# First feed-forward product of six token chunks as seven block products, a key maximum as bias, and a new order table

## The chip, the cores and the metric

The kernel runs on one core of one Trainium2 chip. Its engines work side by side, each through its own instructions in a fixed order: TensorE (PE) multiplies matrices out of SBUF into the eight banks of PSUM, VectorE (DVE) and ScalarE (ACT) work elementwise on either memory, GpSimd (POOL) on SBUF alone, and SyncE (SP) issues the DMA transfers to and from HBM. An instruction starts when the one before it on its engine has started or ended and the semaphores that it waits for have come. The metric is the device time of one execution in microseconds (us); lower is better.

## What is computed

Two stages. Linear attention with an exponential feature map, for 8 batches and 8 heads of 576 positions with 64 dimensions, and then a feed-forward part with a cosine:

```python
def phi(x):
    proj = einsum('bhsd,df->bhsf', x, w_phi)                  # 64 -> 128 features
    proj = proj - max(abs(proj), axis=-1, keepdims=True)
    return concatenate([exp(proj), exp(-proj)], axis=-1)
q_p, k_p = phi(q), phi(k)
kv  = einsum('bhsf,bhsd->bhfd', k_p, v);  z = sum(k_p, axis=2)
attn = einsum('bhsf,bhfd->bhsd', q_p, kv) / (einsum('bhsf,bhf->bhs', q_p, z) + 1e-6)
x = attn as (4608 tokens, 512)
h = x @ w_in                                                  # 512 -> 2048
out = (h * cos(h)) @ w_out                                    # 2048 -> 512
```

All of it is float32 in and out. The feed-forward weights are kept as 64-bit floats by the host and arrive as pairs of words.

## The kernel before

**Attention.** A unit is one batch and two heads; there are 32 units (`attention`, u = 0 to 31). A unit projects queries (L426, L429) and keys (L472, L496), takes the maximum of the absolute values, subtracts it, exponentiates both signs, multiplies with the values (L570, L576), then forms the denominators (L609) and the numerators (L619), and writes its part of x to HBM. For keys the maximum is a reduction on DVE (`k_max`, L508). For units 0 to 7 (`K_SUMS`) it is subtracted by a matmul with minus the unit matrix into the same bank (`k_sub`, L518); for the others by a DVE subtraction (L513). The key parts i = 0 and 1 are 128 x 512, part 2 is a tail of 128 x 128. The exponentials (`exp_k`, L526) then run on ACT, one instruction for a part and a sign. These matmuls have float32 operands, and the profile records each of them as two passes.

**Weights.** `convert` turns 16 tiles of the words (one tile: 128 features of w_in and of w_out) into a high and a low part of a shorter type, so that a product is three matmuls (high x high, low x high, high x low). Three of its operations, each over 1024 columns, are on POOL for tiles 0 to 3 (`W_POOL`) and on DVE for the others. The converted tiles lie in a ring of eight (`w`) and are stored to HBM; `reload` brings them back (1024 KB each).

**Feed-forward.** The 4608 tokens are 9 chunks of 512 (`visit`). Chunks 0 to 2 are visited several times, for a quarter or two of the weights at a time, while attention and conversion go on; chunks 3 to 8 once each, over all 16 weight tiles (stage "n."). For a chunk x is split into a high and a low part (L49 on ACT, L54 on DVE), and for each weight tile of 128 features come: the first product, 12 matmuls of 128 x 512 into one bank (`mm1`, L726: 4 blocks of the 512 inputs, three times); two ACT copies of the bank (`copy`, L732 to an integer number of turns, L733 as it is); `reduce` (DVE, L737), `cosine` (ACT, L741), `times` (DVE, L744), and the split of the result into `high` (ACT) and `low` (DVE); and the second product, 12 matmuls of 128 x 512 into four accumulating banks (`mm2`, L760 to L762). At the end of a chunk the four banks are copied out and stored.

**What sets the order.** Every piece of work is a `Step` with its engine and the steps that it needs. The table `ORDER` lists all steps of all engines in one sequence; each engine runs its own in that sequence, and the eight PSUM banks are given out along it. The number beside each step (its cost) is not used when the program is built. SP issues loads, stores and reloads in the same sequence.

## Time and profile before

| what | value |
|---|---|
| median of 3 runs | 1079.09 us (1079.06 to 1081.62) |
| profiled execution: span | 1079.3 us, 19379 instructions |
| PE matmuls recorded | 7614, of which 1728 in L726 and 1728 in L760 to L762 |
| HBM read, written | 118.55 MB, 41.94 MB |
| DMA packets | 92603, 161.76 MB, mean 150 GB/s |
| ACT table loads | 21 at the cosine, 11 and 9 at the exponentials, 1 at the first copy, 1283 ns each |

The profile has no time of the execution beside its span; the span is from the first instruction to the last. In the views below a row of the timeline is: start in us from the beginning of the span, duration in us, engine, line, operation, what is written <- what is read, and the shape; "PEld" is the weight load, which overlaps the matmuls. Numbers of buffers are left out of names where they tell nothing. A matmul's duration is longer than its share of the engine, since matmuls follow each other in a pipeline; its pitch is the distance of two starts.

### The profile page before, as it was taken

The page shows a single profiled execution, that of the slowest core. Times are in us where ns is not written, and L with a number is a line of the kernel's source. Part 1 is how long each engine was busy: PE and PEld are TensorE (multiplying, and loading weights), DVE is VectorE, ACT ScalarE, POOL GpSimd, SP SyncE. Part 2 cuts the span into 40 slices and gives each one's busy share as a digit, 9 for nine tenths or more (in the row PEclk, how much of TensorE's full clock was granted, in tenths as well). Part 3 has the DMA queues.
Part 4 walks back from the last instruction along what each step waited for, and adds up shares of the span by engine and source line. Part 5 has one row for each costly group of instructions (what it writes and reads, how often), then busy time and mean ns, then how long its engine had stood idle before and what let it go on. Part 6 is the DMA issues. An engine that isn't in the chain of part 4 may idle for free.

```text
span 1079.3 us, 19379 instructions
## 1 busy us (share of the span) xinstructions
PE 1071.7 (99%) x7614; PEld 828.3 (77%) x7614; DVE 704.1 (65%) x1139; ACT 710.7 (66%) x1352; POOL 157.3 (15%) x187
## 2 busy tenths in 40 slices
PE   9999999999999999999999999999999999999998
PEld 6657677787878877788677877786877878888886
DVE  5999999988788767634766556665756343424433
ACT  5898999778666676745676575867467644444442
POOL 3775223000000201101120111120111000000000
PEclk9999999999999999999999999999999999999999
DMA  7564754657655336473132733166312620620441
GB/s 214 174 183 151 221 158 123 199 180 255 219 197 171 118 119 227 177 251 137 54 116 95 234 134 113 41 215 214 97 32 83 232 100 30 244 97 1 174 158 59
DMA packets 92603, 161.76 MB, mean 150 GB/s; under 512 B 43744, under 2 KB 52064, under 8 KB 84320
## 3 DMA queue, kind: packets, MB, share of 16 engines
q1 hardware_dynamic: 92352, 160.46, 44.3%
q8 instruction: 60, 0.98, 0.4%
q14 instruction: 31, 0.25, 0.1%
q10 hardware_dynamic: 160, 0.07, 0.0%
HBM read 118.55 MB, written 41.94 MB: 149 GB/s over the span
## 4 chain that ended last, share of the span: by engine, by line
PE 92%; DVE 0%; issue 0%; DMA 0%; ACT 0%; DVEq 0%
PE bank L726 36%; PE bank L760 12%; PE bank L762 12%; PE bank L761 12%; PE bank L619 5%; PE bank L570 4%; PE bank L609 3%; PE bank L426 2%; PE bank L472 2%; PE bank L576 1%; PE bank L429 1%; PE bank L496 1%; DMA out<-o_last 0%; DVE w_t_f__961 L350 0%; PE bank L518 0%
## 5 line engine op out<-in xcount | busy, mean ns | idle before, releaser
L741 ACT ACT_TABLE_LOAD x21 | 26.9, 1283 | 0.3
L457 POOL COPY m_u__3949<-m_u__3949 32x36 f32<-32x36 f32 x3 | 2.4, 808 | 159.5 <-DVE m_u__3949 L452 159.5
L800 DVE TENSOR_TENSOR o<-bank,o 128x512 f32<-128x512 f32 x24 | 16.2, 684 | 4.0 <-PE bank L762 4.0
L531 ACT ACT_TABLE_LOAD x11 | 14.1, 1283 | 0.2
L726 PE MATMUL bank<-xh_c__5603,w 128*128 128x512 f32 x32 | 13.2, 411 | 0.0
L726 PE MATMUL bank<-xh_c__6807,w 128*128 128x512 f32 x32 | 12.9, 404 | 0.0
L726 PE MATMUL bank<-xh_c__7487,w 128*128 128x512 f32 x32 | 12.8, 399 | 0.0
L726 PE MATMUL bank<-xh_c__4406,w 128*128 128x512 f32 x32 | 12.6, 395 | 0.0
L726 PE MATMUL bank<-xh_c__5779,w 128*128 128x512 f32 x32 | 12.5, 391 | 0.0
L726 PE MATMUL bank<-xh_c__5689,w 128*128 128x512 f32 x32 | 12.5, 391 | 0.0
L726 PE MATMUL bank<-xh_c__6990,w 128*128 128x512 f32 x32 | 12.5, 391 | 0.0
L726 PE MATMUL bank<-xh_c__6870,w 128*128 128x512 f32 x32 | 12.5, 390 | 0.0
L726 PE MATMUL bank<-xh_c__5852,w 128*128 128x512 f32 x32 | 12.5, 390 | 0.0
L726 PE MATMUL bank<-xh_c__8046,w 128*128 128x512 f32 x32 | 12.5, 390 | 0.0
L726 PE MATMUL bank<-xh_c__6988,w 128*128 128x512 f32 x32 | 12.5, 390 | 0.0
L726 PE MATMUL bank<-xh_c__7887,w 128*128 128x512 f32 x32 | 12.5, 390 | 0.0
L726 PE MATMUL bank<-xh_c__4453,w 128*128 128x512 f32 x32 | 12.5, 389 | 0.0
L726 PE MATMUL bank<-xh_c__4662,w 128*128 128x512 f32 x32 | 12.5, 389 | 0.0
L726 PE MATMUL bank<-xh_c__4490,w 128*128 128x512 f32 x32 | 12.5, 389 | 0.0
L726 PE MATMUL bank<-xh_c__7907,w 128*128 128x512 f32 x32 | 12.4, 389 | 0.0
L726 PE MATMUL bank<-xh_c__8323,w 128*128 128x512 f32 x32 | 12.4, 389 | 0.0
L726 PE MATMUL bank<-xh_c__8787,w 128*128 128x512 f32 x32 | 12.4, 389 | 0.0
(3968 smaller groups left out, 4066.7 us busy)
## 6 DMA issues: line engine op xcount, KB each, us to landing
w<-w_parts SPq DMA_DIRECT2D x48, 1024.0 KB, 5.4
w_parts<-w SPq DMA_DIRECT2D x16, 1024.0 KB, 5.7
vmain<-vS SPq DMA_DIRECT2D x32, 256.0 KB, 4.1
out<-o SPq DMA_DIRECT2D x32, 256.0 KB, 2.9
sums<-o SPq DMA_DIRECT2D x24, 256.0 KB, 3.4
o<-sums SPq DMA_DIRECT2D x24, 256.0 KB, 3.0
vtail<-vT SPq DMA_DIRECT2D x64, 16.0 KB, 3.4
out<-o_last SPq DMA_DIRECT2D x4, 256.0 KB, 2.0
```

The costliest lines, as they stand in the source:

```text
L426: PE.matmul(out=bank(qb[j]), lhsT=wphi[r, :], rhs=d["qr"][r, 0:CT], start=True, stop=True)
L472: PE.matmul(out=ps[j][:, P * s:P * s + P], lhsT=x[r, P * s:P * s + P], rhs=wphi[r, :], start=(s == 0), stop=w, skip_group_check=True)
L531: ACT.activation(out=e[:, s, :], in_=d["pq"][:, j * S:(j + 1) * S], func=AF.Exp, scale=1.0 - 2.0 * s)
L570: PE.matmul(out=acc[c:c + 64, n, i, :], lhsT=e[:, s, P * n + c:P * n + c + 64], rhs=vmain[u % 2][:, s, i, :], start=(s == 0 and i == 0 and ...
L609: PE.matmul(out=ps[32 * g:32 * g + 32], lhsT=d["z"][:, 2 * n + j, :], rhs=d["eq", j][:, n, hf * HALF:(hf + 1) * HALF], start=(n == 0), sto ...
L619: PE.matmul(out=d["nps", hf][64 * j:64 * j + 64], lhsT=d["kv"][:, 2 * n + j, :], rhs=d["eq", j][:, n, cut[hf]], start=(n == 0 and hf == 0) ...
L726: PE.matmul(out=h, lhsT=a[:, cs], rhs=d[b, kt], start=(k == 0), stop=(k == 3 * KT - 1))
L741: ACT.activation(out=m["g"], in_=m["g"], func=AF.Sin, bias=halfpi, scale=1.0)
L760: PE.matmul(out=a, lhsT=gh[:, t], rhs=w[:, 0], start=first, stop=False)
L761: PE.matmul(out=a, lhsT=gh[:, t], rhs=w[:, 1], start=False, stop=False)
L762: PE.matmul(out=a, lhsT=gl[:, t], rhs=w[:, 0], start=False, stop=last)
L800: DVE.tensor_tensor(out=o, in0=bank(acc[tb]), in1=o, op=ALU.add)
```

## The change

**The first product in seven.** For chunks 3 to 8 the weight tiles are taken in pairs (256 features), and x and w_in as 2 x 2 blocks: two halves of the 512 inputs, and for x two halves of the 512 tokens, for w_in the two tiles of the pair. Instead of eight block products the kernel makes seven, of sums and differences of blocks, and adds them up in two banks X and Y, as in the Strassen-Winograd scheme. A block product is 6 matmuls of 128 x 256. Copies of half a bank (`snap`) are taken on ACT between products, and two additions (`even`, `odd`) on DVE. Chunks 0 to 2 keep the plain product (`plain_tile`).

```python
def product(bank_b, half, block, name, start, m=m, wi=wi):
    w = w_tiles[wi]
    out = bank(bank_b)[:, half * HC:(half + 1) * HC]
    k = 0
    for part, x in ((0, "h"), (1, "h"), (0, "l")):
        for j in range(2):
            PE.matmul(out=out, lhsT=w[:, part, block, j * P:(j + 1) * P], rhs=d[x, name][:, j * HC:(j + 1) * HC],
                      start=start and k == 0, stop=k == 5, skip_group_check=True)
            k += 1
...
p1 = mul(X, 0, 2, "b11", True, chain["mm1"])
p5 = mul(Y, 1, 5, "t1", True, [p1])
ca = snap(1, 0, X, 0, [p1], True)
cd = snap(0, 1, Y, 1, [p5], True)
p6 = mul(X, 0, 6, "t2", False, [p5, ca])
p3 = mul(Y, 1, 7, "b22", False, [cd])
p2 = mul(Y, 0, 3, "b21", False, [cd])
cb = snap(1, 1, X, 0, [p6], False)
p7 = mul(X, 0, 4, "t3", False, [cb])
...
p4 = mul(X, 0, 1, "t4", False, [c22])
whole = [snap(0, 0, X, 0, [p4, c22], False), odd_row]
```

For x, four differences are made on DVE and seven blocks are split where there were four; each has one buffer, where there were two. ACT makes the turns from the copy in SBUF (`turns`), no longer from the bank. The second product is issued in halves of two banks (6 matmuls) instead of all four.

**The weights.** w_in and w_out have tiles of their own, eight of each (a pair of features' tiles). An input tile has eight blocks, four of w_in and four of sums:

```diff
-    rings.update(w=N1, v=2, kr=2, qr=2, pq=2, bq=1, pk=4, pk_t=2, ek=2, ek_t=2, eq=3, kv=2, rb=2,
-                 x_raw=2, hs=3, g=3, gh=3, gl=3, o=2, w_raw=1, w_t=1)
+    rings.update(wi=3, wo=3, v=2, kr=2, qr=2, pq=2, bq=1, pk=4, pk_t=2, ek=2, ek_t=2, eq=3, kv=2, rb=2,
+                 x_raw=4, hs=4, g=3, gh=3, gl=3, o=2, w_raw=1, w_t=1)
...
-    W_POOL = range(4)
+    W_POOL = ()
+    PLAIN = 9
...
+        def sums():
+            v = d["t1"].bitcast(F32).rearrange("p (h j s c) -> p h s j c", h=2, j=2, s=2)
+            a21, a22, a11, a12 = v[:, 0, 0], v[:, 1, 0], v[:, 0, 1], v[:, 1, 1]
+            for out, x, y, op in ((a22, a21, a22, ALU.add), (a21, a11, a21, ALU.subtract),
+                                  (a11, a22, a11, ALU.subtract), (a12, a12, a11, ALU.subtract)):
+                eng.tensor_tensor(out=out, in0=x, in1=y, op=op)
```

Three tiles of each kind stay in SBUF, so a chunk of the stage "n." reloads five input tiles (seven of the eight blocks, 1792 KB) and five output tiles (1024 KB), 30 of each in all, where 48 tiles of 1024 KB were reloaded.

**The key maximum.** Only parts 0 and 1 of units 0 to 7 keep the matmul (`on_pe`). All others go into the exponential as its bias, which is one number per partition, so that a part of 512 columns becomes four instructions for each sign:

```diff
-            pk = d["pk", i] = new(tag, [P, n, P], F32, f"pk_u{u}_")
-            DVE.tensor_tensor(out=pk, in0=pv, in1=m.unsqueeze(2).broadcast_to([P, n, P]), op=ALU.subtract)
+            if i not in on_pe:
+                l = d["lk", i] = new(tag, [P, n], F32, "lk", "l" + tag)
+                DVE.tensor_scalar(out=l, in0=m, scalar1=-1.0, scalar2=None, op0=ALU.mult)
...
-                ACT.activation(out=e[:, :, s * P:(s + 1) * P], in_=pk, func=AF.Exp, scale=1.0 - 2.0 * s)
+                if i in on_pe:
+                    ACT.activation(out=e[:, :, s * P:(s + 1) * P], in_=pk, func=AF.Exp, scale=1.0 - 2.0 * s)
+                    continue
+                for g in range(n):
+                    ACT.activation(out=e[:, g, s * P:(s + 1) * P], in_=pk[:, g, :], func=AF.Exp, scale=1.0 - 2.0 * s,
+                                   bias=d["lk" if s == 0 else "mk", i][:, g:g + 1])
```

**The order.** `ORDER` is a new table throughout:

```diff
     ORDER = [
-        0, 39, 1, 1128, 15, 3, 2, 14, 20, 21, 4, 6, 5, 24, 16, 18, 54, 41, 17, 42, 19, 53, 43, 22, 45, 23, 44, 1129,
...
```

On PE, in one of the last chunks, the order before goes from the end of a second product (bank 70) to a first product (bank 72); xh and xl are the high and low part of x, gh and gl those of the result, w the weights:

```order
L760 MATMUL bank_70<-w,gh_c__9999 128x512
L761 MATMUL bank_70<-w,gh_c__9999 128x512
L762 MATMUL bank_70<-w,gl_c__10025 128x512
L726 MATMUL bank_72<-xh_c__9119,w 128x512
L726 MATMUL bank_72<-xh_c__9291,w 128x512
L726 MATMUL bank_72<-xh_c__9519,w 128x512
L726 MATMUL bank_72<-xh_c__9436,w 128x512
```

Now, in such a chunk (wi and wo are input and output weights; L954 to L956 are the second product, L857 the block products; xh_b and xh_t are blocks of x and differences of them):

```order
L954 MATMUL bank_74<-wo,gh 128x512
L955 MATMUL bank_74<-wo,gh 128x512
L956 MATMUL bank_74<-wo,gl 128x512
L857 MATMUL bank_70<-xh_b_10830,wi 128x256 x4
L857 MATMUL bank_70<-xl_b_10860,wi 128x256 x2
L857 MATMUL bank_71<-xh_t_10894,wi 128x256 x4
L857 MATMUL bank_71<-xl_t_10900,wi 128x256 x2
L857 MATMUL bank_75<-xh_t_10256,wi 128x256 x4
L857 MATMUL bank_75<-xl_t_10271,wi 128x256 x2
L954 MATMUL bank_69<-wo,gh 128x512
L955 MATMUL bank_69<-wo,gh 128x512
L956 MATMUL bank_69<-wo,gl 128x512
```

A run of 12 long matmuls has become single block products of 6 short ones, set between halves of the second product; the third one here belongs to the pair before.

On ACT, in the first fifth of the program, the exponentials of two units' keys before (ek is their result, pk the keys less their maximum):

```order
L526 ACTIVATE ek_u__2007<-pk_u__1952 128x128 x2
L526 ACTIVATE ek_u__2010<-pk_u__1753 128x4x128 x2
L526 ACTIVATE ek_u__2013<-pk_u__1941 128x4x128 x2
L732 ACTIVATE g_c__2017<-bank_72 128x512
L733 ACTIVATE hs_c__2016<-bank_72 128x512
```

Now (mk is the maximum, lk its negative, wo_t a weight tile in conversion):

```order
L622 ACTIVATE ek<-bank_71,lk 128x128 x4
L622 ACTIVATE ek<-bank_71,mk 128x128 x4
L402 ACTIVATE wo_t_2172<-wo_raw 128x1024
L403 ACTIVATE wo_t_2174<-wo_raw 128x1024
L732 ACTIVATE d_2156<-d_2156 32x9 x4
L622 ACTIVATE ek<-bank_72,lk 128x128
L622 ACTIVATE ek<-bank_72,mk 128x128
L622 ACTIVATE ek<-bank_76,lk 128x128 x4
L622 ACTIVATE ek<-bank_76,mk 128x128 x4
```

Two instructions for a part have become eight, and they read the bank itself, which stays taken until they are done.

On DVE, at the first conversion, before (the three operations that follow stand on POOL):

```order
L348 TENSOR_SCALAR w_t_f__192<-w_t_f__192 128x1024
L350 SCALAR_TENSOR_TENSOR w_t_f__193<-w_raw_f__137,w_t_f__192 128x1024
L352 TENSOR_SCALAR w_t_f__192<-w_t_f__193 128x1024
L451 TENSOR_TENSOR m_u__221<-m_u__181 64x36
L452 TENSOR_TENSOR m_u__222<-m_u__221 32x36
```

Now:

```order
L430 TENSOR_TENSOR wi_t_274<-wi_t_274,wi_t_272 128x1024
L537 TENSOR_REDUCE m_302<-pq 128x18 x2
L602 TENSOR_REDUCE mk<-bank_71 128x4
L602 TENSOR_REDUCE mk<-bank_76 128x1
L605 TENSOR_SCALAR lk<-mk 128x1
L54 TENSOR_TENSOR wi_t_272<-wi_t_273,wi 128x2x4x128
L440 TENSOR_TENSOR wi<-wi_t_272,wi_t_274 128x1024
L545 TENSOR_TENSOR m_418<-m_302 64x36
L546 TENSOR_TENSOR m_419<-m_418 32x36
L721 TENSOR_REDUCE dn<-bank_70 128x9
L723 TENSOR_SCALAR dn<-dn 128x9
L725 RECIPROCAL d_433<-dn 128x18
```

The operations of a tile that were POOL's (L430, L54, L440) stand among DVE's work for the attention, and the sums (L448) follow them.

More of the change, by code (lines that the diff above doesn't have):

```diff
@@ L322, in phi_attention_then_cos_ffn, with convert @@
-    w_ready = {}
-    w_stored = {}
-    def convert(ft):
+    w_shape = {"wi": [P, 2, 8, 2 * P], "wo": [P, 2, 2, DM]}
+    w_parts = {(kind, i): dram.tile(w_shape[kind], F32, name=f"{kind}_parts{i}") for kind in ("wi", "wo") for i in range(NP)}
+    w_tiles, w_slot, w_ready, w_stored = {}, {}, {}, {}
+    def convert(kind, i):
         d = {}
-        slot = w_slot[ft] = Buf("w")
-        name, eng, cost = ("POOL", POOL, 2.4) if ft in W_POOL else ("DVE", DVE, 1.135)
+        me = (kind, i)
+        slot = w_slot[me] = Buf(kind)
+        name, eng, slow = ("POOL", POOL, 2.1) if me in W_POOL else ("DVE", DVE, 1.0)
@@ L495, in k_mm @@
                 ps = d["kps", 2] = bank(d["kb", 2])
[L496 to L497 removed]
+                PE.matmul(out=ps[:, 0:P], lhsT=d["kr"][:, P * NSLOT:P * NSLOT + P], rhs=wphi, start=True, stop=True, skip_group_check=True)
                 return
@@ new lines, in visit, with load @@
+        raw, raw_b, loads = {}, {}, {}
+        for h in range(2):
+            for n in range(2):
+                def load(h=h, n=n):
+                    raw[h, n] = new("x_raw", [P, CT], F32, "x_raw")
+                    if plain:
+                        kt = 2 * h + n
+                        SP.dma_start(out=raw[h, n], in_=xs[kt * P:(kt + 1) * P, c * CT:(c + 1) * CT])
+                        return
+                    SP.dma_start(out=raw[h, n].rearrange("p (j t) -> p j t", j=2),
+                                 in_=xs[h * 2 * P:(h + 1) * 2 * P, c * CT + n * HC:c * CT + (n + 1) * HC].rearrange("(j p) t -> p j t", p=P))
+                x = raw_b[h, n] = Buf("x_raw")
+                rows = [2 * h + n] if plain else [2 * h, 2 * h + 1]
+                chain["x"] = [Step("SP", 0.9, load, [stored[NHP * bt + kt] for bt in batches for kt in rows] + chain["x"],
+                                   take=[x], kind=stage + "load")]
+                loads[h, n] = chain["x"]
@@ new lines, in plain_tile, with mm1, copy @@
+            def plain_tile(r, m, wi, hs):
+                b = Buf("bank")
+                def mm1():
+                    w = w_tiles[wi]
+                    k = 0
+                    for part, x in ((0, "h"), (1, "h"), (0, "l")):
+                        for kt in range(KT):
+                            PE.matmul(out=bank(b), lhsT=w[:, part, 2 * r + kt // 2, kt % 2 * P:(kt % 2 + 1) * P], rhs=d[x, BLOCKS[kt]],
+                                      start=(k == 0), stop=(k == 3 * KT - 1))
+                            k += 1
+                def copy():
+                    m["hs", r] = new("hs", [P, CT], F32, "hs")
+                    m["g", r] = new("g", [P, CT], F32, "g")
+                    ACT.activation(out=m["g", r].bitcast(I32), in_=bank(b), func=AF.Copy, scale=1.0 / TWO_PI, bias=0.25)
+                    ACT.activation(out=m["hs", r], in_=bank(b), func=AF.Copy, scale=1.0)
+                s1 = Step("PE", 2.72, mm1, [ready[k] for k in BLOCKS[:KT]] + w_ready[wi] + chain["mm1"], take=[b, hs[r]],
+                          use=[xb[k] for k in BLOCKS[:KT]] + [w_slot[wi]], kind=stage + "mm1")
+                chain["mm1"] = [s1]
+                return s1, copy, b
@@ L790, in visit @@
+            if c >= GROUP and i < kept:
+                reload("wi", pairs[rings["wi"] + i])
+                reload("wo", pairs[rings["wo"] + i])
         for tb in range(NB3):
```

366 lines of the change are left out of this document (207 added, 159 removed), and 344 rows, old and new, of the table ORDER.

## The prediction

> **What bounds the kernel now.** I read the page from its top: busy time by engine, then the chain that ended last.
>
> ```profile
> PE 1071.7 (99%) x7614; PEld 828.3 (77%) x7614; DVE 704.1 (65%) x1139; ACT 710.7 (66%) x1352; POOL 157.3 (15%) x187
> ...
> PE 92%; DVE 0%; issue 0%; DMA 0%; ACT 0%; DVEq 0%
> PE bank L726 36%; PE bank L760 12%; PE bank L762 12%; PE bank L761 12%; PE bank L619 5%; PE bank L570 4%; PE bank L609 3%; PE bank L426 2%; PE bank L472 2%; PE bank L576 1%; PE bank L429 1%; PE bank L496 1%; DMA out<-o_last 0%; DVE w_t_f__961 L350 0%; PE bank L518 0%
> ```
>
> PE is busy for 99% of the span and makes 92% of the chain; no other engine and no DMA has 1% of it. L726, the first product of the feed-forward part, is 36% of the chain. So a change counts by what it does to the PE's own instruction stream, and by new waits of the PE. A busy PE is not a PE at its peak, so the next view is the pitch of its matmuls late in the program, in order of time (start, duration, line, tiles, shape).
>
> ```profile
> 900.57 0.39 PE L760 MATMUL bank<-w,gh_c__9065 128*128 128x512 f32 x1
> ...
> 911.45 0.39 PE L760 MATMUL bank<-w,gh_c__9191 128*128 128x512 f32 x1
> ```
>
> From 900.57 to 911.45 us there stand 48 matmuls of 512 columns: 10.88 / 48 = 0.2267 us from start to start, without a gap. The row's duration of 0.39 is longer than the pitch, since matmuls overlap. A pair of feature tiles is 2 x 12 such matmuls in the first product, 24 x 0.2267 = 5.44 us. The third view is the busy time of the engines by stretch (PE, weight loads, DVE, ACT, POOL; then the PE clock, the DMA share and GB/s).
>
> ```profile
> 25.00:200.00 175.00, 173.86 (x1951) 119.37 (x1948) 165.70 (x280) 158.85 (x337) 80.95 (x78) 1.00 0.53 162
> 200.00:400.00 200.00, 200.00 (x999) 162.18 (x998) 167.72 (x239) 141.34 (x239) 9.94 (x10) 1.00 0.56 190
> 400.00:1000.00 600.00, 600.00 (x4093) 468.80 (x4092) 328.75 (x555) 365.57 (x699) 58.62 (x75) 1.00 0.39 132
> ```
>
> The granted clock is 1.00 throughout. From 25 to 200 us, where attention, weight conversion and the first visits overlap, DVE is busy 95% and ACT 91% of the time, beside a PE that does not pause; after 400 us DVE is at 55% and ACT at 61%. So the PE sets the end, but in the first fifth two other engines stand close behind it.
>
> The span of this profiled execution is 1079.3 us, 0.2 above the median of the runs shown (1079.09), so nothing of note lies around it, and I make the sum against 1079.3.
>
> **The change, part by part.**
>
> *Seven block products.* Six chunks times eight pairs are 48 places. In each, 24 matmuls of 512 columns (5.44 us) become 7 x 6 = 42 matmuls of 256 columns, each with its own 128x128 weight load. In streamed columns that is 10752 for 12288, seven eighths. What counts is the pitch p of a 256-column matmul of this type, which the trace of before does not show. Half of 0.2267 is 0.1133, the lower bound: 42 x 0.1133 = 4.76, or 0.68 us less per pair, 32.7 us in all. The nearest rows that have two widths are the float32 matmuls of the attention part (each is recorded twice, as two passes):
>
> ```profile
> 29.04 0.39 PE L496 MATMUL bank<-wphi,kr_u__265 128*128 128x128 f32 x2
> 29.27 0.39 PE L429 MATMUL bank<-qr_u__274,wphi 128*128 128x128 f32 x2
> 29.49 0.39 PE L496 MATMUL bank<-wphi,kr_u__275 128*128 128x128 f32 x2
> 29.71 1.03 PE L518 MATMUL bank<-mk_u__396,minus 128*128 128x512 f32 x2
> 30.58 1.02 PE L518 MATMUL bank<-mk_u__400,minus 128*128 128x512 f32 x2
> 31.44 0.38 PE L518 MATMUL bank<-mk_u__412,minus 128*128 128x128 f32 x2
> 31.66 0.59 PE L518 MATMUL bank<-mk_u__408,minus 128*128 128x512 f32 x1
> ```
>
> Six passes of 128 columns take 29.71 - 29.04 = 0.67 us, 0.112 each; the last row gives 0.22 / 2 = 0.110. Four passes of 512 take 31.44 - 29.71 = 1.73, 0.4325 each. A quarter of 0.4325 is 0.108, so the fixed part there is (4 x 0.111 - 0.4325) / 3, about 4 ns, and a column costs (0.4325 - 0.111) / 384, 0.84 ns. With 4 ns fixed here too, p = (0.2267 - 0.004) / 2 + 0.004 = 0.115. The upper bound: if this type streams at just twice their rate, 512 columns are 0.214 us, and the other 12.4 ns are a fixed price of the instruction; then p = 0.107 + 0.0124 = 0.120, 5.04 per pair, 0.40 less, 19.2 us in all. I take 0.115, since these rows have halves and quarters that cost hardly more than their share: 42 x 0.115 = 4.83, 0.61 less per pair, **-29.3 us** in all. The same rows show the weight loads at that pace:
>
> ```profile
> 28.93 0.30 PEld L496 LDWEIGHTS bank<-wphi,kr_u__265 128*128 128x128 f32 x2
> ```
>
> Two loads of 128x128 stand in 0.30 us, and every pass of 0.112 us has one, so a load per 0.115 us is shown.
> The Trainium skill ("TensorE: Matmul & The Clock Gate", section "Back-to-back issue gap") gives a warm gap of N / 2.4 + 2.5 ns, 215.8 ns at 512 columns and 109.2 at 256; by it a pair would lose 5.18 - 4.59 = 0.59 us, 28.5 in all, by way of estimate. The trace disagrees on the size at 512 (226.7) and not on the difference.
>
> *Key maximum as a bias.* The PE loses the small subtraction matmul of the tail of units 0 to 7. The row at 31.44 is one: 0.22 us until the next starts, 8 x 0.22 = **-1.8 us**. On ACT an exponential over 512 columns becomes four over 128, each with its own bias, for both halves of units 8 to 31 (the float32 rows of ACT below, one of 256 columns first):
>
> ```profile
> 66.35 0.39 ACT L584 ACTIVATE kv_u__926<-bank 128x256 f32<-128x256 f32 x1
> 66.61 0.29 ACT L585 ACTIVATE z_u__927<-bank 128x128 f32<-128x128 f32 x1
> 66.77 0.47 ACT L526 ACTIVATE ek_u__930<-bank 128x128 f32<-128x128 f32 x2
> 67.08 1.12 ACT L526 ACTIVATE ek_u__949<-bank 128x512 f32<-128x512 f32 x2
> 68.04 1.14 ACT L526 ACTIVATE ek_u__952<-bank 128x512 f32<-128x512 f32 x2
> ```
>
> Two 512-column exponentials take 68.04 - 67.08 = 0.96; the 128-column ones step by 0.155, so eight take 1.24, +0.28 per half, and at most, at the 0.29 of the lone copy at 66.61, 2.32, +1.36. DVE loses the subtractions and gains three small negations:
>
> ```profile
> 98.69 0.69 DVE L513 TENSOR_TENSOR pk_u__1275<-bank,mk_u__1273 128x512 f32<-128x512 f32 x1
> 99.30 1.43 DVE L443 TRANSPOSE_TENSOR_REDUCE m_u__1252<-pq_u__1253 128x18 f32<-128x576 f32 x2
> ...
> 101.73 0.17 DVE L627 TENSOR_SCALAR dn_u__1337<-dn_u__1337 128x9 f32<-128x9 f32 x1
> ```
>
> The subtraction steps by 0.61, a small operation by some 0.17: -1.2 - 0.2 + 0.5 = -0.9 us per unit.
>
> *Weights.* Four tiles' conversions go from POOL to DVE, 12 operations; each input tile gets four sums, one more copy on ACT and one more subtraction on DVE. The price of such a DVE operation:
>
> ```profile
> 184.65 1.18 DVE L54 TENSOR_TENSOR w_t_f__1875<-w_t_f__1875,w 128x1024 f32<-128x1024 f32 x1
> 185.75 0.68 DVE L508 TENSOR_REDUCE mk_u__2506<-bank 128x4 f32<-128x512 f32 x1
> ```
>
> 1.10 us for 1024 columns, a quarter for a sum of 256. In the stretch from 25 to 200 us stand half the conversions (8 of 16 in either order), so DVE gets 12 x 1.10 + 4 x (4 x 0.28 + 1.10) = 13.2 + 8.9 = 22, less 8 units x 0.9 = 7: 165.7 + 15 = 181 of 175 us. ACT gets 16 halves x 0.28 to 1.36 and 4 copies of 1024 columns (twice 0.48): 158.9 + 8 to 26. Both are then at or just over the stretch, and what they are over is a wait of the PE: 0 to 10 us. I take **+3**: in before a DVE at 95% costs the PE nothing that its rows show, POOL's conversions no longer run beside DVE's, and the sums are needed only after 400 us.
>
> *Order.* The new order leaves the PE's full-array shapes for the tiled ones (64 rows, 64 or 32 columns) 57 times where the old one did 38 times. The price, out and back:
>
> ```profile
> 103.39 0.50 PE L760 MATMUL bank<-w,gh_c__1232 128*128 128x512 f32 x1
> 103.72 0.39 PE L761 MATMUL bank<-w,gh_c__1232 128*128 128x512 f32 x1
> ...
> 108.73 0.39 PE L762 MATMUL bank<-w,gl_c__1335 128*128 128x512 f32 x1
> 109.05 1.13 PE L426 MATMUL bank<-qr_u__1166,wphi 64*128 64x512 f32 x4
> ```
>
> L762 to L426 takes 0.32 instead of 0.227, and after the return L760 to L761 takes 0.33: 0.2 us a time, 19 x 0.2 = **+4** (3 to 6, since the first step of the return may cost another 0.1).
>
> *What lies beside other work.* In the chunk stage ACT makes four half-bank copies (0.26 each by the row at 66.35) and two conversions for four full copies, and DVE two more additions per pair: some 1 us more in 10 us, on engines that are 55 to 61% busy. The copies are now in the PE's way: a product into a half-bank waits until ACT has read the one before. The PE's order puts another product and a half of the second product (1.36 us) between; the round trip is the matmul's overhang (0.39 - 0.23), the copy's 0.39 and two handovers, under 0.8. If ACT runs an exponential or a table load first, that cover is gone and a wait of up to 1 us follows; queued behind it on the PE are all later matmuls. I count nothing for it in the middle case.
>
> *Reloads.* 30 input tiles of 1792 KB and 30 output tiles of 1024 KB are read again, where 48 of 1024 KB were:
>
> ```profile
> w<-w_parts SPq DMA_DIRECT2D x48, 1024.0 KB, 5.4
> ...
> o<-sums SPq DMA_DIRECT2D x24, 256.0 KB, 3.0
> ```
>
> From 256 KB to 1024 KB it is 2.4 us more, so 1792 KB land in some 7.8 us. In the new order at least 9 us of matmuls stand between the last reader of the old tile and the first of the new, mostly 11 to 30. Nothing is counted, and SP's queue, which these issues share, has only x loads and stores ahead of them.
>
> Sum: -29.3 - 1.8 + 3 + 4 = -24.1; 1079.3 - 24.1 = **1055.2 us**.
>
> **The rivals.**
> *Fixed price per matmul.* If the 12.4 ns belong to the instruction and not to its columns, p = 0.120 and the sum is -19.2 - 1.8 + 7 = -14: 1065.3. For it: 0.2267 is more than twice the float32 rate explains, so something is special to this type; against it: the float32 rows show a fixed part of 4 ns only. Chance 0.15.
> *DVE and ACT become the bound before 200 us.* The sum above leaves them 6 us over; with all of it and of ACT's upper price, +10 in place of +3: 1062 to 1066. For it speaks the 95%; against it that after 200 us there is room. Chance 0.13.
> *A late tile.* A reload that lands beside an output tile's shares the queue: 2816 KB take 11 us at 2.4 us per 768 KB. At the six or so tightest places that is 2 to 3 us of wait each: +15, 1070. The DMA share of 0.39 after 400 us speaks against it. Chance 0.05.
> *The weight load sets the pitch, and the kernel is slower.* At half the columns a load may no longer hide:
>
> ```profile
> 900.80 0.19 PEld L762 LDWEIGHTS bank<-w,gl_c__9090 128*128 128x128 f32 x1
> ```
>
> Such a load takes 0.19 us. If the next could start only when it is done, p = 0.19: 42 x 0.19 = 7.98, +2.54 per pair, +122 in all, and the end near 1206. It decides from p = 0.126 on, where the pair's gain no longer pays the +5 of the other terms. Against it: the passes at 0.112 us in the rows from 29.04 on, each with its own load. The Trainium skill (same page, Part 3, "The mechanism") says that a weight load overlaps running matmuls only where the row group differs; by that rule no 128-row load here could hide. The trace disagrees: the load at 900.80 runs inside the matmuls around it, at a pitch of 0.2267. Chance 0.04.
>
> **How the numbers follow.** My forecast, p near 0.115 with waits of a few us, 1048 to 1062, has 0.62; the rivals 0.15, 0.13, 0.05 and 0.04; 0.01 is left for a change that does nothing (the same number of streamed columns), which the built order excludes. Low end: 32.7 + 1.8 - 3 = 31.5, 1047.8. High end: p = 0.120 with early waits of 10 gives -19.2 - 1.8 + 14 = -7, 1072. The range is 1047.5 to 1071; it leaves out the slow rival and the ends. A measurement of this kernel can tell about 0.3%, 3.2 us, from no change. Only the slow rival and a sum of several late tiles reach 1076: faster 0.93, same 0.02, slower 0.05.
>
> **What would show it.** In the profile of the changed kernel: the pitch of L857's rows (0.113 to 0.116 for the forecast, 0.120 for the first rival, near 0.19 for the last); their total in the chain near 48 x 4.83 = 232 us, for 261 of L726 in the same six chunks; the PE's idle time before 200 us by the engine that ended it; PE rows after 400 us without gaps above 0.3 us, where a wait would name ACT's half-bank copy or a reload of an input tile. Wrong would be the step on the pitch if L857's mean step lies outside 0.113 to 0.120, and the step on the covers if the PE loses more than 10 us in waits.

## Result and the profile after

The changed kernel takes 1082.40 us (median of 11 runs, 1081.09 to 1083.94) beside 1080.46 us for the kernel before (median of 11, 1078.82 to 1081.71): a ratio of 1.0019, 95% interval 1.0010 to 1.0028. That is slightly slower, by less than the 0.3% of the prediction, and 27 us above its 1055.2. The profiled execution took 1081.13 us, with a span of 1079.0 (1079.3 before), at a granted clock of 1.00. Every execution that was recorded with its span took 1.7 to 2.2 us more than the span.

The page of the changed kernel, busy time and the chain that ended last:

```profile
PE 1061.1 (98%) x8462; PEld 850.1 (79%) x8462; DVE 781.3 (72%) x1337; ACT 833.2 (77%) x1794; POOL 145.2 (13%) x175
...
PE 81%; ACT 8%; DVE 7%; DMA 1%; issue 1%; SPq 1%; ACTq 0%; DVEq 0%
PE bank L857 21%; PE bank L954 11%; PE bank L955 11%; PE bank L956 11%; PE bank L905 10%; PE bank L715 4%; PE bank L666 4%; PE bank L705 2%; ACT ek L622 2%; PE bank L566 2%; PE bank L520 2%; ACT eq L628 1%; PE bank L672 1%; DVE mk L602 1%; PE bank L610 1%
```

PE is busy for 10.6 us less than before, and its share of the chain has fallen from 92% to 81%: ACT has 8% and DVE 7%, where they had nothing. So work was saved, and waits took its place. The pitch, in order of time:

```profile
904.81 0.64 PE L857 MATMUL bank<-xh_b,wi 128*128 128x256 f32 x4
905.28 0.40 PE L857 MATMUL bank<-xl_b,wi 128*128 128x256 f32 x2
905.52 0.64 PE L857 MATMUL bank<-xh_b,wi 128*128 128x256 f32 x4
906.00 0.40 PE L857 MATMUL bank<-xl_b,wi 128*128 128x256 f32 x2
906.25 0.64 PE L857 MATMUL bank<-xh_t,wi 128*128 128x256 f32 x4
906.73 0.40 PE L857 MATMUL bank<-xl_t,wi 128*128 128x256 f32 x2
906.97 0.64 PE L857 MATMUL bank<-xh_t,wi 128*128 128x256 f32 x4
```

From 904.81 to 906.97 us start 18 matmuls of 256 columns: 2.16 / 18 = 0.120 us, the upper bound of the prediction and not its 0.115. The stretches (busy us of PE, weight loads, DVE, ACT, POOL; then the clock, the DMA share and GB/s), and what PE waited for (in all, times, longest):

```profile
25.00:200.00 175.00, 168.37 (x1828) 110.22 (x1824) 160.28 (x284) 163.57 (x396) 51.78 (x59) 1.00 0.57 186
200.00:400.00 200.00, 200.00 (x1144) 160.33 (x1142) 182.05 (x268) 165.35 (x286) 19.14 (x17) 1.00 0.59 208
400.00:1000.00 600.00, 595.32 (x4827) 498.51 (x4826) 386.11 (x698) 451.50 (x1012) 63.18 (x75) 1.00 0.54 186
```

```profile
PE bank L715 <- DVE dn L721: 3.8, 6, 0.7
PE bank L905 <- ACT ek L622: 3.0, 2, 1.6
PE bank L905 <- DVE rb L740: 1.5, 2, 0.8
...
PE bank L566 <- ACT ek L622: 0.9, 1, 0.9
PE bank L956 <- DVE gl L54: 0.9, 1, 0.9
```

Before 200 us PE has lost 5.5 us more than in the kernel before (168.37 for 173.86), and between 400 and 1000 us, where it had no pause at all before, 4.7 us. Over these 175 us DVE is not over its bound: 160.3 us, less than the 165.7 before. The second half of the stretch looks different, first before, then after:

```profile
100.00:200.00 100.00, 100.00 (x1131) 71.94 (x1128) 94.56 (x169) 91.85 (x192) 29.05 (x36) 1.00 0.52 157
100.00:200.00 100.00, 94.75 (x934) 64.44 (x932) 87.92 (x147) 94.18 (x239) 25.28 (x29) 1.00 0.60 203
```

Between 100 and 200 us the chain that ended last lay on PE alone before. Now, its pieces added up, 44 us of it are ACT's, 25 DVE's and 22 PE's.

To see where the whole 24 us went I took, for every step on PE, the time from its start to that of the next, and split it into the shortest such time for two steps of these kinds (for the matmuls of the feed-forward part, their number times the pitch) and the rest, which is waiting. In us, summed over the program:

| part | predicted | measured, after less before |
|---|---|---|
| seven products for eight, 48 x (5.44 - 42 p) | -29.3 (p = 0.115) | -19.2 (p = 0.120) |
| tail subtractions on PE | -1.8 | -1.9 |
| more changes between full and tiled shapes | +4 | +4.1 |
| waiting, 0 to 200 us | +3 | +6.9 (11.4 to 18.3) |
| waiting, 200 to 400 us | 0 | +0.3 |
| waiting from 400 us on | 0 | +9.7 (7.8 to 17.5) |
| sum | -24.1 | -0.1 |

The table is about the two profiled executions, whose spans differ by -0.3 us; the medians differ by +1.9. Two terms failed: the pitch (10.1 us) and the waits (13.9 us). Most of these waits stand in a few gaps. From 80 us on (the start differs from run to run) one single step of the kernel before took over 0.3 us longer than the shortest of its kind (0.5 us); in the changed kernel there are 16, 15.7 us together.

### The profile page after: what moved, and what is told of

It is laid out like the page before. It is cut to its first block, busy times and chain, and to the rows that moved or that the text cites. A ratio compares the mean times of both kernels' runs of the same rounds, so it can differ in the third digit from the quotient of the medians.

```text
span 1079.0 us, 21627 instructions
## 1 busy us (share of the span) xinstructions
PE 1061.1 (98%) x8462; PEld 850.1 (79%) x8462; DVE 781.3 (72%) x1337; ACT 833.2 (77%) x1794; POOL 145.2 (13%) x175
## 4 chain that ended last, share of the span: by engine, by line
PE 81%; ACT 8%; DVE 7%; DMA 1%; issue 1%; SPq 1%; ACTq 0%; DVEq 0%
PE bank L857 21%; PE bank L954 11%; PE bank L955 11%; PE bank L956 11%; PE bank L905 10%; PE bank L715 4%; PE bank L666 4%; PE bank L705 2%; ACT ek L622 2%; PE bank L566 2%; PE bank L520 2%; ACT eq L628 1%; PE bank L672 1%; DVE mk L602 1%; PE bank L610 1%
## 5 line engine op out<-in xcount | busy, mean ns | idle before, releaser
L954 PE MATMUL bank<-wo,gh 128*128 128x512 f32 x576 | 228.7, 397 | 0.0
L955 PE MATMUL bank<-wo,gh 128*128 128x512 f32 x576 | 225.7, 392 | 0.0
L956 PE MATMUL bank<-wo,gl 128*128 128x512 f32 x576 | 224.6, 390 | 0.9 <-DVE gl L54 0.9
L869 ACT ACTIVATE hs<-bank 128x256 f32<-128x256 f32 x192 | 70.6, 384 | 97.6 <-PE bank L857 87.4
L931 DVE SCALAR_TENSOR_TENSOR g<-g,hs 128x512 f32<-128x512 int32 x144 | 102.7, 725 | 43.2 <-ACT g L927 34.3
L956 PEld LDWEIGHTS bank<-wo,gl 128*128 128x128 f32 x576 | 108.2, 188 | 25.0 <-DVE gl L54 1.3
L938 DVE TENSOR_TENSOR g<-hs,g 128x512 f32<-128x512 f32 x144 | 101.2, 709 | 36.8 <-ACT g L935 36.3
L54 DVE TENSOR_TENSOR gl<-g,gh 128x512 fp32r<-128x512 f32 x144 | 100.5, 703 | 37.8 <-ACT gh L49 37.2
L954 PEld LDWEIGHTS bank<-wo,gh 128*128 128x128 f32 x576 | 108.6, 189 | 24.3 <-issue 4.2
L559 POOL TENSOR_TENSOR pq<-pq,bq 128x576 f32<-128x576 f32 x64 | 101.4, 1604 | 178.4 <-DVE bq L555 164.4
L857 PE MATMUL bank<-xh_t,wi 128*128 128x256 f32 x768 | 124.3, 284 | 0.0
L935 ACT ACTIVATE g<-g,halfpi 128x512 f32<-128x512 f32 x144 | 101.9, 719 | 27.3 <-DVE g L931 26.6
L955 PEld LDWEIGHTS bank<-wo,gh 128*128 128x128 f32 x576 | 108.7, 189 | 17.2
L857 PEld LDWEIGHTS bank<-xh_t,wi 128*128 128x128 f32 x768 | 110.5, 190 | 11.1 <-issue 1.7
L857 PE MATMUL bank<-xh_b,wi 128*128 128x256 f32 x576 | 93.4, 284 | 0.0
L905 PE MATMUL bank<-xh_b,wi 128*128 128x512 f32 x288 | 82.9, 396 | 4.5 <-ACT ek L622 3.0
L857 PEld LDWEIGHTS bank<-xh_b,wi 128*128 128x128 f32 x576 | 81.6, 191 | 6.2 <-DVE g L938 1.5
L857 PE MATMUL bank<-xl_t,wi 128*128 128x256 f32 x384 | 77.3, 283 | 0.0
```

Source lines behind the costliest of these rows:

```text
L54: eng.tensor_tensor(out=out, in0=in_, in1=hi.bitcast(F32), op=ALU.subtract)
L559: qeng.tensor_tensor(out=d["pq"][:, c], in0=d["pq"][:, c], in1=d["bq"][:, c], op=ALU.subtract)
L857: PE.matmul(out=out, lhsT=w[:, part, block, j * P:(j + 1) * P], rhs=d[x, name][:, j * HC:(j + 1) * HC], start=start and k == 0, stop=k == ...
L905: PE.matmul(out=bank(b), lhsT=w[:, part, 2 * r + kt // 2, kt % 2 * P:(kt % 2 + 1) * P], rhs=d[x, BLOCKS[kt]], start=(k == 0), stop=(k == 3 ...
L931: DVE.scalar_tensor_tensor(out=g, in0=g.bitcast(I32), scalar=-TWO_PI, in1=m["hs", r], op0=ALU.mult, op1=ALU.add)
L935: ACT.activation(out=n["g"], in_=n["g"], func=AF.Sin, bias=halfpi, scale=1.0)
```

## Experiments

The table gives, for each timed kernel, the median, the ratio to the kernel before (95% interval) and the gaps of over 0.3 us on PE. The kernel before had medians of 1080.5 to 1081.7 in the four comparisons, so differences below 2 us are read from the gaps. In two of the profiles the granted clock is 0.5 for 3.4 us: in "subtraction back" from 152.2 us, in "moves, units 8 and 13" from 188.3 us. In each, some 1.7 us of the early gaps are that clock and not a wait.

| kernel | us | ratio | gaps 80 to 200 us | gaps from 200 us |
|---|---|---|---|---|
| before | 1080.46 | | 1, 0.5 us | 0 |
| changed | 1082.40 | 1.0019 (1.0010 to 1.0028) | 8, 9.0 | 8, 6.7 |
| subtraction back | 1088.79 | 1.0075 (1.0061 to 1.0088) | 10, 12.5 | 11, 9.2 |
| numerators ahead of inversion | 1079.46 | 0.9984 (0.9975 to 0.9993) | 8, 8.4 | 4, 4.6 |
| POOL converts | 1086.09 | 1.0044 (1.0030 to 1.0057) | 10, 11.2 | 8, 6.7 |
| no sums | 1080.79 | 0.9990 (0.9981 to 0.9999) | 7, 7.7 | 8, 6.7 |
| before, eight for two | 1102.38 | 1.0188 (1.0172 to 1.0205) | 12, 12.7 | 9, 8.5 |
| order moves | 1079.56 | 0.9984 (0.9974 to 0.9994) | 11, 9.1 | 4, 3.3 |
| moves, units 8 and 13 | 1078.25 | 0.9974 (0.9964 to 0.9985) | 10, 8.2 | 4, 3.3 |
| late moves, unit 8 | 1076.87 | 0.9964 (0.9951 to 0.9976) | 5, 6.3 | 4, 3.2 |
| no shift | 1075.87 | 0.9954 (0.9941 to 0.9968) | 6, 3.7 | 7, 5.9 |
| no shift, no sums | 1075.10 | 0.9951 (0.9936 to 0.9966) | 5, 3.3 | 7, 5.9 |

### 1. The pitch by itself

```diff
+        for n in (512, 384, 320, 256, 192, 128, 64):
+            for k in range(24):
+                PE.matmul(out=banks[0][:, 0:n], lhsT=pw[:, k % 3 * P:(k % 3 + 1) * P], rhs=px[:, 0:n], ...)
```

> The kernel before, with runs of 24 fp32r matmuls ahead of its own work (two passes over twelve or more shapes), so its time is some 60 to 80 us longer and says nothing; only the pitch of the added line counts. Two pitches are known from the changed kernel, 226.7 ns at 512 columns and 120 ns at 256, so 0.4167 ns a column and 13.3 ns that do not shrink. Theory A, a fixed price of each matmul: 173.3 ns at 384 columns, 93.3 at 192, 66.7 at 128, 40 at 64, and the same 120 ns at 256 columns with 64 columns of weights, with one weight tile used again, and with two banks in turn. Theory B, the 128-column weight load sets the pitch at 256 columns: 120 ns at 256 columns and about as much at 192, 128 and 64, and less than 115 ns with half as many weight columns. Theory C, an accumulation into one bank costs the 13.3 ns: 107 ns with two banks in turn or with two halves of a bank in turn, 120 ns otherwise.

1181.74 us, one execution, 100 us longer than before. The last two runs of 24, two banks in turn (L852) and two halves of a bank in turn (L855), and the row behind them:

```profile
102.59 3.04 PE L852 MATMUL bank<-px,pw 128*128 128x256 f32 x24
105.47 3.04 PE L855 MATMUL bank<-px,pw 128*128 128x256 f32 x24
108.35 0.39 PE L496 MATMUL bank<-wphi,kr_u__808 128*128 128x128 f32 x2
```

2.88 / 24 = 0.120 us both times, so theory C falls. The median distances of two starts in the second pass, in ns:

| weight columns | 512 | 384 | 320 | 256 | 192 | 128 | 64 |
|---|---|---|---|---|---|---|---|
| 128 | 227 | 173 | 147 | 120 | 111 | 111 | 112 |
| 64 | 229 | | | 113 | | 59 | |

(At 512 with 64 weight columns the mean is 231, with steps of up to 265.) One weight tile used again gives 120 at 256 columns as well. Theory A holds from 256 columns up: 0.4167 ns a column and 13.3 ns. Below, it is theory B's kind of limit, but at 111 and not at 120: as far as these runs tell, a load of 128 weight columns comes through every 0.111 us, for with 64 weight columns 128 columns go at 59 ns. At 256 columns the fixed part is smaller with 64 weight columns, 113 - 106.7 or some 6 to 7 ns; at 512 it is not. With half the weight columns the product has half the output rows too, and the two were not told apart. So 256 columns stand just above the floor, and the seven products lose 42 x 13.3 where the eight lost 24 x 13.3.

### 2. The subtraction back on VectorE

```diff
-                l = d["lk", i] = new(tag, [P, n], F32, "lk", "l" + tag)
-                DVE.tensor_scalar(out=l, in0=m, scalar1=-1.0, scalar2=None, op0=ALU.mult)
+                DVE.tensor_tensor(out=pv, in0=pv, in1=m.unsqueeze(2).broadcast_to([P, n, P]), op=ALU.subtract)
...
-                if i in on_pe:
+                if True:
```

> The changed kernel with the maximum taken off again by VectorE (in place in the bank) and two exponentials of 512 columns in place of eight of 128 with a bias, in the same order of steps; the seven products stay. Theory ACT, the eight exponentials (0.249 us apart, so 1.99 us a part in place of 0.96) hold the banks and make TensorE wait between 90 and 200 us: the waits of the plain first product on these exponentials (3.0 us) go, of the 10.9 us lost between 100 and 200 us at least 5 go, and the time falls by 4 to 8 us, to 1074 to 1078. Theory DVE, VectorE is the bound there (160 of 175 us busy): 0.53 us more on VectorE for each of about 30 parts before 200 us makes it slower by 5 to 12 us, 1087 to 1094. If neither engine sets the waits, 1081 to 1084.

1088.79 us, 6.4 slower than the changed kernel. The stretch up to 200 us, and its longest waits (L714, L904 and L955 are L715, L905 and L956 of the changed kernel):

```profile
25.00:200.00 175.00, 166.01 (x1811) 109.42 (x1808) 165.13 (x283) 146.63 (x310) 52.42 (x60) 0.99 0.54 176
```

```profile
PE bank L714 <- DVE dn L720: 5.8, 8, 2.1
PE bank L904 <- DVE rb L739: 3.0, 2, 2.3
PE bank L520 <- DVE o L1001: 1.7, 1, 1.7
PE bank L955 <- DVE gl L54: 1.4, 1, 1.4
```

ACT lost 17 us and DVE gained 5; the releasers are now DVE's. The three gaps that the expectation named for ACT shrank from 1.51, 1.73 and 1.66 to 0.65, 0.60 and 0.48 us, 3.2 us less, so the eight exponentials do hold PE there; but the others grew, or came, by 9.2 us. Part of that is the clock, which fell right behind PE's wait of 2.3 us (L904, up to 151.16 us):

```profile
152.20:155.60 3.40, 3.40 (x9) 2.30 (x7) 3.37 (x6) 0.81 (x3) 3.06 (x2) 0.50 0.91 320
```

That costs some 1.7 us here, and all five executions of this kernel have a mean clock of 0.994 to 0.998, the changed kernel 0.999 to 1.000. Why it fell is not shown. The time goes with theory DVE. So going back to the subtraction does not save the change: in this order the kernel is slower still.

### 3. The numerators ahead of the inversion

```diff
-        z_mm, invert, ..., n_mm        (six units, steps 300, 708, 844, 980, 1014, 1116)
+        z_mm, n_mm, invert, ...
```

> The changed kernel with six pairs of steps turned round in its order: where the numerators follow the denominators on TensorE with nothing between and VectorE's inversion stands between them in the order, the numerators are put ahead of the inversion. Nothing else moves. Theory ORDER, the 0.66 to 0.75 us between the two at 105, 534, 638, 741, 778 and 869 us are a wait of the numerators for the inversion that reads the same bank, made by the order alone: all six go to 1.11 us from start to start, and the time falls by 4.1 us, to about 1078.3. Rival, TensorE would have waited there or right behind for something else: the time falls by less than 1 us, 1081.4 to 1082.8.

One of the six, first in the changed kernel, then here (L694, L704 and L710 are its L705, L715 and L721):

```profile
741.38 1.18 PE L705 MATMUL bank<-eq,z 128*32 128x288 f32 x16
...
742.63 0.48 DVE L721 TRANSPOSE_TENSOR_REDUCE dn<-bank 128x9 f32<-128x288 f32 x1 [2.39 <-PE bank L705]
...
743.16 1.31 PE L715 MATMUL bank<-eq,kv 128*64 128x64 f32 x12 [0.61 <-DVE dn L721]
```

```profile
742.11 1.18 PE L694 MATMUL bank<-eq,z 128*32 128x288 f32 x16
...
743.21 1.31 PE L704 MATMUL bank<-eq,kv 128*64 128x64 f32 x12
...
743.71 0.48 DVE L710 TRANSPOSE_TENSOR_REDUCE dn<-bank 128x9 f32<-128x288 f32 x1 [2.76 <-PE bank L704]
```

From start to start 1.78 us became 1.10: the numerators write the bank that the inversion reads, and wait for it when the table puts it first. All six waits went. In the place at 638 us another came, 1.3 us at 644, where the inversion had to be moved with its successor, so 2.9 us were gained and not 4.1. Theory ORDER holds for five of the six. In the table of before the inversion always stands behind the numerators where PE makes the two without a step between.

### 4. GpSimd converts the first tiles

```diff
-    W_POOL = ()
+    W_POOL = tuple((kind, i) for kind in ("wi", "wo") for i in range(2))
```

> The changed kernel with the conversion of the first two pairs of weight tiles (rest, low, add, sums and the sums' low part, some 20 us of VectorE) done by GpSimd, in the same order of steps. Theory DVE, VectorE (160 of 175 us busy between 25 and 200 us, after taking these over) makes TensorE wait: VectorE falls to about 142 us there, and the time falls by 3 to 7 us. Theory ACT, ScalarE sets these waits: no gain, between 0 and 6 us slower, since GpSimd takes about twice as long for each step and the first plain product needs the tiles.

1086.09 us, 3.7 slower, in the range of theory ACT. The gaps from 98 us on are those of the changed kernel, each within 0.05 us; two new ones (0.51 and 1.56) stand before. DVE's busy time up to 200 us fell by only 3 us:

```profile
25.00:200.00 175.00, 166.09 (x1795) 109.53 (x1792) 157.38 (x260) 160.51 (x385) 83.93 (x79) 1.00 0.55 178
```

Before 100 us DVE was relieved by 4.4 us (68.0 for 72.4), from 100 to 200 us not at all (89.4 for 87.9). So the load of the early conversions on DVE before 100 us is not what makes the gaps from 98 us on; that ACT's load makes them does not follow.

### 5. Without the sums of weight blocks

```diff
-            for out, x, y, op in ((a22, a21, a22, ALU.add), ...):
-                eng.tensor_tensor(out=out, in0=x, in1=y, op=op)
+            pass
```

> The changed kernel without the sums of weight blocks: for each of the eight pairs of w_in, VectorE's four sums (0.42 us each) and their low part (1.2 us) and ScalarE's high part (about 1 us) are left out, and the products that would read a sum read a plain block, so the outputs are not the reference's; the stores write the plain blocks twice, with the same bytes. Three of the pairs are converted before 200 us: 8.6 us less on VectorE and 3 us less on ScalarE there. Theory LOAD, the gaps of TensorE between 100 and 200 us (10.9 us) come from too much work on these two engines: they fall to 7 or less, and the time by 3 to 6 us, to 1076 to 1079. Rival LOCAL, each gap comes from one step that stands in a wrong place of the order, and what else the engine does matters little: only the gap at 145 us, where the sums stand on VectorE ahead of the step that frees the bank, goes (0.8 us), and the time falls by 0.5 to 2 us, to 1080.5 to 1082.

1080.79 us, 1.6 less than the changed kernel, in the range of rival LOCAL. By the ratios to the kernel before (0.9990 and 1.0019) it is some 3 us less, the edge of theory LOAD, so the gaps must decide, and they are for LOCAL. The gap at 145 us is gone (0.82), the one at 94.6 us shrank by 0.5, and the others stayed, with 8.6 us less work on DVE. ACT stays 94% busy between 100 and 200 us.

### 6. Eight exponentials for two in the kernel before

```diff
-            DVE.tensor_tensor(out=pk, in0=pv, in1=m.unsqueeze(2).broadcast_to([P, n, P]), op=ALU.subtract)
+            DVE.tensor_copy(out=pk, in_=pv)
...
+                for g in range(n):
+                    ACT.activation(out=e[:, g, s * P:(s + 1) * P], in_=pk[:, g, :], func=AF.Exp, scale=1.0 - 2.0 * s,
+                                   bias=d["lk" if s == 0 else "mk", i][:, g:g + 1])
```

> The kernel before with one part of the change alone, and only its cost: from unit 8 on, ScalarE takes eight exponentials of 128 columns with a bias in place of two of 512 for each large part, and VectorE copies the bank to SBUF and negates the maximum in place of the subtraction, so VectorE and the banks keep their times. About 14 such parts lie before 200 us: 14 times 1.03 us more on ScalarE, 158.9 to about 173 of the 175 us. Theory ACT, ScalarE is near enough to its bound for that to reach TensorE: 5 to 10 us slower than before, 1085 to 1091. Rival, its idle time takes it: within 2 us of before, 1079 to 1083.

1102.38 us: 20.7 slower than before, twice the end of the expected range. Some 11.5 us of waiting were added between 100 and 200 us and the rest later. Between 100 and 200 us ACT is 97% busy, and 61 us of the chain there are ACT's. Two stretches, and three of PE's longest waits:

```profile
100.00:200.00 100.00, 91.48 (x1007) 64.43 (x1006) 83.86 (x162) 97.37 (x248) 28.81 (x36) 1.00 0.49 154
400.00:1000.00 600.00, 594.48 (x4056) 463.31 (x4057) 332.36 (x593) 405.66 (x891) 58.29 (x75) 1.00 0.39 135
```

```profile
PE bank L580 <- ACT o L817: 2.7, 2, 1.5
PE bank L736 <- ACT pq_u__4449 L437: 1.6, 1, 1.6
PE bank L619 <- ACT z_u__1878 L595: 1.5, 1, 1.5
```

PE waits for copies that share ACT's queue with the exponentials. So theory ACT has the mechanism right before 200 us. But in this order the 1.03 us more a part reach PE after 400 us as well, with ACT 68% busy; whether another order of the old kernel would take them was not tried.

### 7 to 9. Moves in the order, and single units

Run 7 changes the order alone, in ten places; run 8 also puts the subtraction back for two units (`BACK`); run 9 keeps of both what acted.

Numbers are those of steps in the table:

```diff
+        370 ahead of 1344, 573 ahead of 1875, 302 ahead of 347, 1310 ahead of 1317, 2194 ahead of 796     (run 9: 573 alone)
...
+            if u in BACK and i < 2:                # run 8: (8, 13); run 9: (8,)
+                DVE.tensor_tensor(out=pv, in0=pv, in1=m.unsqueeze(2).broadcast_to([P, n, P]), op=ALU.subtract)
+            elif i not in on_pe:
```

> The changed kernel with ten places of its order changed and no operation: the numerators ahead of the inversion at five of the six places of the earlier run (not at 638 us, where the wait only moved on to 644 us), and on VectorE the step that TensorE waits for put ahead of one to eight others: the numerators' product that frees a bank for the plain first product (at 145 and 401 us) and for the query projection (114 us), the low part of g (124 us), and the copy of an output (563 us). Theory ORDER, these gaps are places of the order and not load: 3.5 us at the five, 0.8 at 145, 1.3 at 401, 0.4 at 114, 0.9 at 124 and 0.7 at 563 go, 7.6 us in all, so 1074 to 1076. Rival LOAD, what is taken from one gap comes back in the next: 1078 or more.

1079.56 us, by its time in the range of rival LOAD. After 200 us the gaps fell from 6.7 to 3.3 us (401 us from 1.84 to 1.01; the one at 563 us only moved on). Before 200 us nothing was won: the gap at 124 us (1.16) became four, 0.63, 0.45, 0.43 and 0.33, and the one at 145 us came back as 0.87 at 151 us. There rival LOAD holds, later theory ORDER.

> As the run with ten places of the order changed, and for units 8 and 13 alone the maximum is taken off by VectorE in place in the bank, with two exponentials in place of eight for each large part. Theory HELD, the gaps at 94.6, 181.5 and 188.8 us (1.51, 1.73 and 1.66 us) are waits for banks and values that the eight exponentials of these units hold: with the subtraction put back everywhere they were 0.65, 0.60 and 0.48 us, so some 3 us less than the run without it, 1071 to 1073. Rival DVE, the 0.53 us more on VectorE for each of the four parts comes out elsewhere: no difference, or up to 2 us more.

1078.25 us, 1.3 less than run 7 and far from theory HELD's 1071 to 1073. Unit 8 was worth it, since the gaps at 96.7, 105.4 and 110.7 us (1.24, 0.64 and 0.65) are gone; unit 13 gained little: those at 183.6 and 190.9 us fell by 0.9, and a new one of 1.62 came between them, where PE waits for DVE's copy of an output. What is left at 190.9, and another of 0.80 behind it, stand where the clock is 0.5 (188.3 to 191.8 us); the profile shows no wait of PE there.

> The changed kernel with what held in the last two runs and nothing else: the numerators ahead of the inversion at five places, the numerators' product two steps earlier on VectorE at 401 us, and the subtraction back on VectorE for unit 8 alone. The other moves before 200 us, which only shifted a gap, and unit 13 are left as in the changed kernel. Of the gaps, the five (3.5 us), 0.8 of the 1.84 us at 401, and with unit 8 those at 94.6 and 103.6 us (1.51 and 0.68) go: 6.5 us, so 1075 to 1077 if each gap is local. If gaps before 200 us only wander, as after the moves at 124 and 145 us, the gain of unit 8 comes back and it is 1078 to 1080.

1076.87 us, 0.9964 of the kernel before: inside the range for gaps that are local, and faster than both, by 4.2 and 5.5 us. Of the 15.7 us in gaps 9.5 are left; PE's two longest waits (L897, L614 and L948 are L905, L622 and L956):

```profile
PE bank L897 <- ACT ek L614: 1.6, 1, 1.6
PE bank L948 <- DVE gl L54: 1.2, 1, 1.2
```

### 10 and 11. No shift of the keys, and no sums either

```diff
-                l = d["lk", i] = new(tag, [P, n], F32, "lk", "l" + tag)
-                DVE.tensor_scalar(out=l, in0=m, scalar1=-1.0, scalar2=None, op0=ALU.mult)
...
-                if i in on_pe:
+                if True:
```

> The changed kernel without the shift of the keys by their maximum in all parts that TensorE doesn't shift: no negation on VectorE, no bias, two exponentials of 512 columns straight from the bank; the maximum is still taken. The outputs are not the reference's. It takes ScalarE's 1.03 us a large part away and puts nothing on VectorE in its place. Theory ACT, the eight exponentials make the gaps between 100 and 200 us: 10.9 falls to 5 or less, and the time by 6 to 9 us, to 1073 to 1076. Rival, most of them are made by releases on VectorE, and the subtraction put back raised them only by its own load: only the gaps at 94.6, 181.5 and 188.8 us shrink, by 3 us, to 1079.

1075.87 us, 6.5 less than the changed kernel. The gap at 181.5 us, in the changed kernel and here (L902, L616 and L953 are L905, L622 and L956):

```profile
182.59 0.39 PE L956 MATMUL bank<-wo,gl 128*128 128x512 f32 x1
184.55 0.96 PE L905 MATMUL bank<-xh_b,wi 128*128 128x512 f32 x3 [1.57 <-ACT ek L622]
...
181.03 1.28 ACT L622 ACT_TABLE_LOAD   x1 [3.82 <-DVE lk L605]
182.32 1.14 ACT L622 ACTIVATE ek<-bank,lk 128x128 f32<-128x128 f32 x4
183.34 1.16 ACT L622 ACTIVATE ek<-bank,mk 128x128 f32<-128x128 f32 x4
```

```profile
181.49 0.39 PE L953 MATMUL bank<-wo,gl 128*128 128x512 f32 x1
181.72 0.84 PE L902 MATMUL bank<-xh_b,wi 128*128 128x512 f32 x3
...
178.84 1.28 ACT L616 ACT_TABLE_LOAD   x1 [3.86 <-DVE mk L602]
180.14 1.42 ACT L616 ACTIVATE ek<-bank 128x512 f32<-128x512 f32 x4
```

At this gap it is a chain of latency and not a full engine: ACT has stood idle for 3.82 us until the negative of DVE's maximum came, loads its table, and then reads the bank eight times until some 184.3 us; the first product, next on PE, needs that bank. In the kernel before the subtraction had moved the keys to SBUF and set the bank free ahead of the exponentials. Without the eight the gap is gone. They are not all of it: here the table load also starts 2.65 us ahead of the second product's last row, and in the changed kernel 1.56, and run 10 leaves out DVE's negation (0.17 us) as well. Of 9.0 us in early gaps 3.7 stay, so the exponentials account for somewhat more than half. Between 100 and 200 us ACT is now 85% busy, and 10 us of the chain are ACT's. Run 10 thus takes away ACT's load and the long last link at once, and which of the two made the other gaps is not told apart. The time is inside its range though the waiting between 100 and 200 us fell to 7.1 us only, not to 5.

> Both left out, the shift of the keys and the sums of weight blocks; outputs are not the reference's. Theory LOAD: with 8.6 us less on VectorE and some 20 us less on ScalarE before 200 us, hardly a gap of over 0.3 us is left between 80 and 200 us, and the time is 1069 to 1073. Rival LOCAL: the run without the sums lost 1.6 us, so this one is 1 to 2 us below the run without the shift, and gaps of over 0.5 us stay at steps whose releasing step stands late in the order (105 us, 114 us, 124 us).

1075.10 us, 0.8 less than run 10: rival LOCAL. With ACT and DVE both relieved, gaps of 0.75, 0.69 and 0.94 us stay at 103, 112 and 122 us; the first of them is the place that run 3 cleared by the order alone.

## Why the prediction was wrong

- **The bound.** Over the program it held: PE is 98% busy at a clock of 1.00. Between 100 and 200 us it did not: there 70 of 100 us of the chain lie on ACT and DVE.
- **The base.** That "nothing of note lies around it" was wrong by some 2 us: times are 1.7 to 2.2 us above spans, and 1079.3 was a span, so the forecast's 1055.2 is one too.
- **The pitch.** This is the first step that failed: "With 4 ns fixed here too, p = (0.2267 - 0.004) / 2 + 0.004 = 0.115". It carried a fixed part over from float32 passes of 128 and 512 columns. Run 1 gives 13.3 ns for this type, from 256 columns up, and 111 ns at 64, 128 and 192 columns alike. The 0.112 us of the 128-column passes is the same number, so those rows probably showed the pace of the loads, from which no fixed part can be read (the float32 passes were not measured by themselves). The first rival had p = 0.120 by the right mechanism, a fixed price (it put 12.4 ns), with a chance of 0.15. Only the term's size was off: 48 x 0.40 = 19.2 us and not 29.3.
- **The Trainium skill on the pitch.** The Trainium skill ("TensorE: Matmul & The Clock Gate", section "Back-to-back issue gap") gives N / 2.4 + 2.5 ns for an isolated matmul. At both widths the measured pitch is 10.8 ns above that, so the difference between the widths agrees and the constant is not that of these matmuls.
- **The weight load.** It does not set the pitch at 256 columns, but its 111 ns are close beneath the 120: at 192 columns, where the columns alone with the 13.3 ns would take 93, the pitch is 111, probably the load's.
- **The early waits, +3.** The second step that failed, in its size (+6.9) and more in its mechanism. It compared sums of busy time with the stretch (DVE 181, ACT 167 to 185 of 175 us). Both came out lower, 160.3 and 163.6, with only 3 of the 8 pairs of tiles of each kind converted before 200 us, where half had been counted, and PE waited all the same. The average over 175 us also hid the stretch from 100 us on, where ACT is 94% busy and the largest part of the chain is ACT's. The exponential's price was inside its bounds: four in 1.00 us (the rows at 182.32 and 183.34 are within 2% of that), so 1.99 for eight and +1.03 per half, between +0.28 and +1.36. What was left out is where these eight stand: the last link from DVE's maximum over a table load to the release of a bank. The rows at 181.5 us show that link, and in runs 2, 8 and 10 gaps behind it shrink or go. Runs 4 and 5, with 3 to 9 us less on DVE up to 200 us, leave nearly all the gaps in place. How much is the link and how much ACT's load stays open.
- **The order, +4.** For the changes of shape it was right (4.1). But it took the table's price to be these changes alone. The waits that the new table makes after 400 us (9.7 us) had been counted as nothing: 3.5 us are five inversions ahead of their numerators (run 3; at one of the five another wait took the place), 0.8 of the 1.84 at 401 us one step on DVE (run 7). The rest was not traced to a cause: what is left at 401 us, the gap at 563 us, where PE waits for DVE's copy of an output and which only moved on in run 7, the one at 655 us, and many of about 0.1 us.
- **Half-bank copies and reloads.** Counted as nothing, and rightly: no row of PE's waits names L869 or a reload. The prediction's sign for this step being wrong, more than 10 us of waits, came true all the same, through other waits. The input tiles land in 8.2 us (7.8 expected):

```profile
wi<-wi_parts SPq DMA_DIRECT2D x30, 1792.0 KB, 8.2
```

- **The range.** Its high end joined p = 0.120 with 10 us of early waits. The sum needed the late waits as well, and the only rival that had late waits (a late tile) had them from reloads.

Open remain 3.3 us of early gaps that neither the exponentials nor the sums explain.

## What to carry to other kernels

A matmul cut in two costs its fixed price twice: measure the pitch of the very type, width and weight tile that will run, since seven eighths of the columns were here 93% of the time (5.04 of 5.44 us). An engine's load over a long stretch does not tell what it costs: ACT was busy for 163.6 of 175 us, stood idle for 3.8 us ahead of the gap at 181.5 us, and PE still waited for it there, through one long step at the end of a chain. So ask of each longer step which bank or buffer it holds and who takes that next, and look at the chain by stretch. A new order table has a price of its own: look in it for steps that read what the next matmul writes.
